# The last two of 231 expert units behind a branch on the routing table

## The chip, the cores and the metric

One core of a Trainium2 chip. The time is the device time of the program in microseconds, the median over several executions; the span is 1.7 to 2.1 us shorter than the time of the same execution. All executions below are on record as fast, none in a slower state. The kernels of this study ran in four jobs, the last three of them on three different chips. One of these is slower than the others by 1.1% (the kernel before takes 1394 us there), so a time is only compared with runs of the kernel before from the same job. A "load" below is the set of runs of one kernel under one label in one job; one execution of each label was traced.

## The reference, cut to what matters

A seven-tap causal convolution along the sequence, with one set of taps for each of 8 groups of channels, makes `attn_out`. A router then picks one expert out of 8 for every token, and the token goes through that expert's two layers.

```python
# batch 8, seq 3584, d_model 192, 8 experts, F = 1024: 28672 tokens, all float32
logits = np.einsum('bsd,de->bse', x, w_gate)
local_gate = 1.0 / (1.0 + np.exp(-np.einsum('bsd,de->bse', x, w_local).squeeze(-1)))
...
        fresh_e = int(np.argmax(logits[b, s]))
        if s == 0 or local_gate[b, s] < 0.5:
            e = fresh_e
        else:
            e = prev_e if prev_e >= 0 else fresh_e
        ...
        h = np.maximum(x[b, s] @ w1[e], 0.0)
        out[b, s] = p[e] * (h @ w2[e])
```

How many tokens an expert gets depends on the data.

## The kernel before

The kernel convolves and routes in 16 groups of 1792 tokens and scatters each routed row into a slot of its expert in a table in memory (`slots`). The slots are worked through in units of 128 rows: 35 single units early, then 87 pairs, then 22 single units at the end (`REST`). The count of 231 covers the worst case, in which each of 8 experts leaves a unit partly filled; a unit that the data does not need gets the entry `DUMMY`, whose rows carry an index out of range.

```python
UT = 128
CAPU = N // UT
NU = (N + E * (UT - 1)) // UT          # 231
DUMMY = E * CAPU
...
    blocks = [(0, 1, i, next(g for g in range(NPART) if i < ONE[g])) for i in range(ONE[-1])]
    blocks += [(1, 2, i, next(g for g in range(NPART) if i < TWO[g])) for i in range(TWO[-1])]
    blocks += [(2, 1, i, NPART - 1) for i in range(REST)]

    def entry(i, col, most):            # SyncE reads the table into a register
        kind, n, at, group = blocks[i]
        return nc.values_load(tabi[kind, group][at:at + 1, col:col + 1], engines=[ET.SP], ...)
    # load_w(i), load_rows(i): DMAs from SyncE, addressed by entry(i, 1, ...) and entry(i, 0, ...)
...
    def hidden(n, wb, xT):              # 48 matmuls for a single unit, then ReLU on ScalarE
    ...
    def output(n, wb, xg, hT):          # 32 matmuls for a single unit
        ...
        for k in range(n):
            nc.scalar.activation(o_sb[:, k, :], y[k][0], Act.Copy, scale=xg[:, k, 0:1])
        step(1.2)
        for k in range(n):
            nc.vector.scalar_tensor_tensor(o_sb[:, k, :], y[k][1], xg[:, k, 0:1], o_sb[:, k, :],
                                           Alu.mult, Alu.add)
            nc.gpsimd.nop()
            sent = nc.gpsimd.indirect_dma_start(out=out, in_=o_sb[:, k, :], ...,
                bounds_check=N - 1, oob_is_err=False)
...
    for i, (_, n, _, _) in enumerate(blocks):
        ensure(i)                       # rows of the next units
        weights(i + AHEAD)              # weights of the next units, 1.5 MB each
        hT = hidden(n, wbs[i], xT)
        if i + 1 < len(blocks):
            xT, copied = turn(blocks[i + 1][1], xgs[i + 1])   # transposes of the next unit
            ...
        output(n, wbs.pop(i), xgs.pop(i), hT)
```

Of the kernel before, what the change touches and what calls it, by code (L numbers as in the profile page):

```python
# [38 lines left out]
NU = (N + E * (UT - 1)) // UT  # L39
DUMMY = E * CAPU  # L40
EARLY = 3


def _sure(tokens, size):

    return max(0, -(-(tokens - E * (size - 1)) // size))



ONE = [_sure(min(g + 1, EARLY) * PT, UT) for g in range(NPART)]  # L50
TWO = [_sure((g + 1) * PT - ONE[-1] * UT, BT) if g >= EARLY else 0 for g in range(NPART)]
REST = NU - ONE[-1] - 2 * TWO[-1]
# [34 lines left out]
def kernel(  # L87
# [8 lines left out]
    nc = tc.nc  # L96
# [173 lines left out]
    tabi = {}  # L270
# [288 lines left out]
    def put(behind=None):  # L559


        if not to_put:
            return
        g, rows, to = to_put.pop(0)
        nc.gpsimd.nop()
        ins = nc.gpsimd.indirect_dma_start(  # L566
            out=slots[:, :], in_=rows, in_offset=None,
            out_offset=bass.IndirectOffsetOnAxis(ap=to, axis=0)).ins
        if behind is not None:
            tc.add_manual_dep(ins, behind.ins.name, SYNC, reason="scatters apart")  # L570
        if puts:
            tc.declare_no_dep(ins, group="puts", reason="slots of their own")
        if g:
            tc.declare_no_dep(ins, group="gets", reason="those slots were full before")
        puts.append((g, ins))
        tc.add_to_no_dep_group("puts", ins)
        tc.add_to_no_dep_group(f"puts{g}", ins)
# [98 lines left out]
    blocks = [(0, 1, i, next(g for g in range(NPART) if i < ONE[g])) for i in range(ONE[-1])]  # L676
# [36 lines left out]
    def turn(n, xg):  # L713


        xps = xps_p.tile([P, 2, 512], F32, name="xps")
        at = xps[:, :, :KD * BT // 2].rearrange("p h (d k s) -> p h d k s", d=KD, k=KT)
        for d in range(KD):
            for k in range(n):
                src = xg[:, k, Y0 + d * DR:Y0 + (d + 2) * DR]  # L720
                for half in range(2):
                    turn_half(at[:, half, d, k, :], src, half)
        xT = tp.tile([P, KD, BT], F32, name="xT")
        to = xT.rearrange("p d (k h s) -> p h d k s", k=KT, h=2)
        if n == KT:
            to, at = [a.rearrange("p h d k s -> p h (d k) s") for a in (to, at)]
        else:
            to, at = [a[:, :, :, 0, :] for a in (to, at)]
        copied = nc.scalar.copy(to, at)  # L729
        return xT, copied  # L730

    def hidden(n, wb, xT):
        hT = hp.tile([P, FK, BT], F32, name="hT")
        w = slice(0, n * P)


        for two in range(2):
            hps = [hps_p.tile([P, 2, BT], F32, name="hps") for half in range(2)]
            for d in range(KD):
                for j in range(2):  # L740
                    f0 = (d * 4 + two * 2 + j) * P
                    for half, rows in halves():
                        nc.tensor.matmul(hps[half][:, j, w], lhsT=wb[rows, f0:f0 + P],  # L743
                                         rhs=xT[rows, d, w], start=(d == 0 and j == 0),
                                         stop=(d == KD - 1), skip_group_check=True)
            for half in range(2):
                m = half * 4 + two * 2
                relu = nc.scalar.activation(hT[:, m:m + 2, w], hps[half][:, :, w], Act.Relu)  # L748
            put(relu)
        return hT  # L750

    def output(n, wb, xg, hT):

        yps = [yps_p.tile([P, 512], F32, name="yps") for half in range(2)]
        for m4 in ([0, 1, 4, 5], [2, 3, 6, 7]):
            for k in range(n):
                for m in m4:
                    for half, rows in halves():
                        nc.tensor.matmul(yps[half][:, k * D:(k + 1) * D],  # L759
                                         lhsT=hT[rows, m, k * P:(k + 1) * P],  # L760
                                         rhs=wb[rows, WA + m * D:WA + (m + 1) * D],
                                         start=(m == 0 and k == 0), stop=(m == FK - 1),
                                         skip_group_check=True)
        o_sb = op.tile([P, KT, D], F32, name="o_sb")
        y = [[yps[half][:, k * D:(k + 1) * D] for half in range(2)] for k in range(n)]
# [9 lines that stand above are left out]
            sent = nc.gpsimd.indirect_dma_start(  # L775
                out=out, in_=o_sb[:, k, :], in_offset=None,
                out_offset=bass.IndirectOffsetOnAxis(ap=xg.bitcast(I32)[:, k, 1:2], axis=0),
                bounds_check=N - 1, oob_is_err=False)
            tc.declare_no_dep(sent.ins, group="sent", reason="each token has one slot")
            tc.add_to_no_dep_group("sent", sent.ins)  # L780
# [5 lines left out]
    def start_conv(on_pe=()):  # L786
        g = st["conv"] + 1

        free = not any(p[0] <= g - 3 for p in to_put)
        if st["cgen"] is None and g < NPART and g <= st["route"] + LEAD and free:  # L790
            st["conv"] = g
            st["cgen"], st["pgen"] = conv(g, x_in.pop(g), on_pe)
            next(st["cgen"])
            if g + 1 < NPART:
                x_in[g + 1] = load_x(g + 1)

    def conv_op():
        c = next(st["cgen"], None) if st["cgen"] else None
        if c is None:
            st["cgen"] = None  # L800
        return c

    def start_route(alone=False):
        done = st["conv"] - (st["cgen"] is not None)
        if st["rgen"] is None and st["route"] < done:
            st["route"] += 1
            st["rgen"] = route(st["route"], alone)

    def route_op():
        c = next(st["rgen"], None)  # L810
        if c is None:
            st["rgen"] = None
            st["routed"] = st["route"]
        return c

    def step(time):

        start_route()
        start_conv()
        go = st["rgen"] is not None  # L820
        while time > 0:
            c = route_op() if go else conv_op()
            if c is None:
                if not go:
                    break
                go = False
            elif c == "hop":
                go = False
            elif c == "placed":
                pass  # L830
            elif c == "pe":
                c = conv_op()
                time -= c or 0
            else:
                time -= c
# [30 lines left out]
    def ensure(i):  # L866

        for j in range(len(xgs) + i, min(i + AHEAD + 1, len(blocks))):
            g = blocks[j][3]
            while st["routed"] < g or any(p[0] <= g for p in to_put):  # L870
                if j > i + 2:
                    return
                step(4.2)
                put()
            xgs[j] = load_rows(j)

    def weights(upto):
        for j in range(loaded[0], min(upto + 1, len(blocks))):
            if (blocks[j][0], blocks[j][3]) not in tabi:
                return  # L880
            wbs[j] = load_w(j)
            loaded[0] += 1

    loaded = [0]
    weights(0)
    for j in range(2):
# [2 lines left out]
    xT, _ = turn(blocks[0][1], xgs[0])  # L889
    for i, (_, n, _, _) in enumerate(blocks):  # L890
        ensure(i)
        weights(i + AHEAD)
        hT = hidden(n, wbs[i], xT)
        if i + 1 < len(blocks):
            xT, copied = turn(blocks[i + 1][1], xgs[i + 1])
            if len(to_put) > NT // 2 and n == KT:
                put(copied)
        step(2.5 if n == 1 else 4.2)
        output(n, wbs.pop(i), xgs.pop(i), hT)
        step(1.3 if n == 1 else 3.0)  # L900


def _w1_layout(np, w1):
# [44 lines left out]
```

## Time and profile before

| | before |
|---|---|
| time | 1378.5 us (three runs, 1378.44 to 1379.59) |
| span of the profiled run | 1377.1 us |
| TensorE busy | 1341.6 us, 97% |
| one single unit of the tail | 5.52 us on TensorE |
| last matmul to the end | 1370.88 to 1377.1 us, so 6.2 us |

The part that matters is the end, and there two intervals: the period of a unit, and the tail between the last matmul and the end. In the tail the last unit is evicted (`o_sb<-yps`, ScalarE and VectorE, 0.42 us each), scattered (GpSimd, 0.97 us), the scatter lands (SyncE's wait for it ends 1.12 us after the scatter's instruction), GpSimd drains (a closing instruction of its sequencer, DRAIN, that in the kernel before begins ahead of the last scatter and ends 3.27 us after it), and a closing barrier joins the engines. The prediction shows the lines.

### The profile page before, as it was taken

The page shows a single profiled execution, that of the slowest core. Times are in us where ns is not written, and L with a number is a line of the kernel's source. Part 1 is how long each engine was busy: PE and PEld are TensorE (multiplying, and loading weights), DVE is VectorE, ACT ScalarE, POOL GpSimd, SP SyncE. Part 2 cuts the span into 40 slices and gives each one's busy share as a digit, 9 for nine tenths or more (in the row PEclk, how much of TensorE's full clock was granted, in tenths as well). Part 3 has the DMA queues.
Part 4 walks back from the last instruction along what each step waited for, and adds up shares of the span by engine and source line. Part 5 has one row for each costly group of instructions (what it writes and reads, how often), then busy time and mean ns, then how long its engine had stood idle before and what let it go on. Part 6 is the DMA issues. An engine that isn't in the chain of part 4 may idle for free.

```text
span 1377.1 us, 42248 instructions
## 1 busy us (share of the span) xinstructions
PE 1341.6 (97%) x17314; PEld 1267.5 (92%) x17314; DVE 794.8 (58%) x2461; ACT 516.0 (37%) x1158; POOL 483.7 (35%) x515
## 2 busy tenths in 40 slices
PE   6789999999999999999999999999999999999998
PEld 4488999999999999999999999999999999999998
DVE  6769999987768686868687778784300000000000
ACT  3234444434333343334333333333333333333333
POOL 1442444434343444444443434343443211112111
PEclk9889999999999999999999999999999999999999
DMA  4299999987676767676767676565665555547993
GB/s 180 100 379 366 379 381 373 365 346 270 207 263 213 263 224 260 229 264 224 263 214 260 213 260 227 204 232 204 225 218 199 195 202 198 180 168 271 320 329 129
DMA packets 66483, 344.16 MB, mean 250 GB/s; under 512 B 12528, under 2 KB 23655, under 8 KB 45810
## 3 DMA queue, kind: packets, MB, share of 16 engines
q1 hardware_dynamic: 44064, 288.76, 58.5%
q0 software_dynamic: 22224, 52.70, 10.1%
q8 instruction: 136, 2.23, 0.6%
q14 instruction: 57, 0.47, 0.1%
q10 hardware_dynamic: 2, 0.00, 0.0%
HBM read 288.61 MB, written 53.49 MB: 248 GB/s over the span
## 4 chain that ended last, share of the span: by engine, by line
PE 62%; issue 22%; DVE 6%; POOL 4%; DMA 4%; ACT 1%; POOLq 0%; SPq 0%; DVEq 0%; ACTq 0%
PE yps L759 28%; PE hps L743 27%; POOL out_dram L775 4%; DVE y_sb L206 3%; DMA xg<-slots 3%; PE xps L278 2%; PE hps L350 2%; PE hps L189 1%; PE yps L189 1%; POOL slots L566 1%; DVE z L340 1%; DVE o_sb L771 1%; DMA x_sb<-in_x_dram 1%; DMA out_dram<-o_sb,xg 0%; ACT z L307 0%
## 5 line engine op out<-in xcount | busy, mean ns | idle before, releaser
L759 PE MATMUL yps<-wb,hT 64*128 64x192 f32 x7392 | 644.0, 326 | 3.2 <-DVE o_sb L771 1.9
L743 PE MATMUL hps<-xT,wb 64*128 64x256 f32 (+1 forms) x6912 | 635.5, 336 | 0.6 <-ACT xT L729 0.6
L759 PEld LDWEIGHTS yps<-wb,hT 64*128 64x128 f32 x7392 | 606.1, 188 | 8.1 <-issue 4.0
L743 PEld LDWEIGHTS hps<-xT,wb 64*128 64x128 f32 x6912 | 573.7, 188 | 39.8 <-ACT xT L729 0.8
L775 POOL DMA_INDIRECT out_dram<-o_sb,xg x231 | 233.5, 1011 | 674.0 <-DVE o_sb L771 601.3
L206 DVE SCALAR_TENSOR_TENSOR y_sb<-x_sb,c,y_sb 128x336 f32<-128x336 f32 x720 | 405.0, 571 | 27.5 <-ACT y_sb L181 8.2
L748 ACT ACTIVATE hT<-hps 128x512 f32<-128x512 f32 (+1 forms) x576 | 263.9, 510 | 364.0 <-PE hps L743 363.8
L771 DVE SCALAR_TENSOR_TENSOR o_sb<-yps,xg,o_sb 128x192 f32<-128x192 f32 x231 | 88.0, 413 | 500.9 <-ACT o_sb L767 495.8
L566 POOL DMA_INDIRECT slots<-y_sb,posi x224 | 223.0, 995 | 185.5 <-ACT hT L748 88.5
L767 ACT ACTIVATE o_sb<-yps,xg 128x192 f32<-128x192 f32 x231 | 87.6, 418 | 425.4 <-PE yps L759 421.8
L729 ACT COPY xT<-xps 128x768 f32<-128x768 f32 (+1 forms) x144 | 97.9, 680 | 10.4 <-PE xps L278 10.4
L278 PEld LDWEIGHTS xps<-ident,xg 64*128 64x128 f32 x1386 | 71.3, 140 | 12.9 <-issue 2.9
L278 PE MATMUL xps<-ident,xg 64*128 64x64 f32 x1386 | 72.8, 222 | 4.9 <-DMA xg<-slots 4.9
L181 ACT ACTIVATE y_sb<-x_sb,c 128x336 f32<-128x336 f32 x116 | 66.7, 586 | 0.0
L340 DVE STREAM_TRANSPOSE z<-y_sb 128x768 f32<-128x768 f32 (+1 forms) x56 | 45.5, 853 | 0.5
L366 DVE COPY lt<-lq 32x36 f32<-32x36 f32 x224 | 41.5, 185 | 3.5
L350 PE MATMUL hps<-z,wg 64*32 64x128 f32 x1344 | 26.9, 274 | 1.9 <-DVE z L340 1.7
L350 PEld LDWEIGHTS hps<-z,wg 64*32 64x32 f32 x1344 | 20.8, 105 | 5.5 <-DVE z L340 3.5
L189 PE MATMUL hps<-x_sb,wb 128*128 128x336 f32 x56 | 18.7, 502 | 3.9 <-DMA x_sb<-in_x_dram 3.9
L189 PEld LDWEIGHTS hps<-x_sb,wb 128*128 128x128 f32 x56 | 12.1, 217 | 10.2 <-issue 5.8
L189 PE MATMUL yps<-x_sb,wb 128*128 128x336 f32 x56 | 19.2, 500 | 0.0
L189 PEld LDWEIGHTS yps<-x_sb,wb 128*128 128x128 f32 x56 | 11.6, 215 | 5.4 <-issue 1.3
(165 smaller groups left out, 336.6 us busy)
## 6 DMA issues: line engine op xcount, KB each, us to landing
wb<-in_w_dram SPq DMA_DIRECT2D x144, 1536.0 KB
x_sb<-in_x_dram SPq DMA_DIRECT2D x16, 1920.0 KB
xg<-slots SPq DMA_DIRECT2D x87, 258.0 KB
xg<-slots SPq DMA_DIRECT2D x57, 129.0 KB
out_dram<-o_sb,xg POOLq DMA_INDIRECT x231
slots<-y_sb,posi POOLq DMA_INDIRECT x224
wg<-in_wgl_dram SPq DMA_DIRECT2D x1, 144.0 KB
slots<-pad SPq DMA_DIRECT2D x1, 129.0 KB
```

The costliest lines, as they stand in the source:

```text
L189: nc.tensor.matmul(acc, lhsT=dg_of(i, k), rhs=chans(h, k), start=(k == 0), stop=(k == KC - 1))
L206: nc.vector.scalar_tensor_tensor(cols(h), chans(h, k), c[:, h, k:k + 1], cols(h), Alu.mult, Alu.add)
L278: nc.tensor.transpose(to, src[rows], identity=ident[rows, rows])
L350: nc.tensor.matmul(lps[half][Q * j:Q * j + Q, :], lhsT=wgq[rows, b, :], rhs=z[rows, begin[j]:begin[j] + TQ, b * Q:(b + 1) * Q], start=(b = ...
L566: ins = nc.gpsimd.indirect_dma_start(out=slots[:, :], in_=rows, in_offset=None, out_offset=bass.IndirectOffsetOnAxis(ap=to, axis=0)).ins
L729: copied = nc.scalar.copy(to, at)
L743: nc.tensor.matmul(hps[half][:, j, w], lhsT=wb[rows, f0:f0 + P], rhs=xT[rows, d, w], start=(d == 0 and j == 0), stop=(d == KD - 1), skip_g ...
L748: relu = nc.scalar.activation(hT[:, m:m + 2, w], hps[half][:, :, w], Act.Relu)
L759: nc.tensor.matmul(yps[half][:, k * D:(k + 1) * D], lhsT=hT[rows, m, k * P:(k + 1) * P], rhs=wb[rows, WA + m * D:WA + (m + 1) * D], start= ...
L767: nc.scalar.activation(o_sb[:, k, :], y[k][0], Act.Copy, scale=xg[:, k, 0:1])
L771: nc.vector.scalar_tensor_tensor(o_sb[:, k, :], y[k][1], xg[:, k, 0:1], o_sb[:, k, :], Alu.mult, Alu.add)
L775: sent = nc.gpsimd.indirect_dma_start(out=out, in_=o_sb[:, k, :], in_offset=None, out_offset=bass.IndirectOffsetOnAxis(ap=xg.bitcast(I32)[ ...
```

## The change

Any routing of 28672 tokens needs 224 to 231 units, so up to seven may be dummies; the last two go behind a branch. All engines read the table entry of the first of them and skip both if it is `DUMMY`.

```diff
--- before.py
+++ after.py
@@ -39,6 +39,7 @@
 NU = (N + E * (UT - 1)) // UT
 DUMMY = E * CAPU
 EARLY = 3
+SPARE = 2
 
 
 def _sure(tokens, size):
@@ -881,6 +882,8 @@
             wbs[j] = load_w(j)
             loaded[0] += 1
 
+    spare = blocks[len(blocks) - SPARE:]
+    del blocks[len(blocks) - SPARE:]
     loaded = [0]
     weights(0)
     for j in range(2):
@@ -898,6 +901,19 @@
         step(2.5 if n == 1 else 4.2)
         output(n, wbs.pop(i), xgs.pop(i), hT)
         step(1.3 if n == 1 else 3.0)
+
+    kind, _, at, group = spare[0]
+    any_left = nc.values_load(tabi[kind, group][at:at + 1, 0:1], min_val=0, max_val=DUMMY,
+                              skip_runtime_bounds_check_because="an entry of the table")
+    with tc.If(any_left < DUMMY):
+        for block in spare:
+            blocks.append(block)
+            i = len(blocks) - 1
+            n = block[1]
+            xg = load_rows(i)
+            wb = load_w(i)
+            xT, _ = turn(n, xg)
+            output(n, wb, xg, hidden(n, wb, xT))
 
 
 def _w1_layout(np, w1):
```

The builder makes two paths of it: the body, and a skip path on which each engine adds to its semaphores what the body would have added, so that later waits can be constants.

## The prediction

> **What bounds the kernel now.** I read the page's first two parts, then the stretches of its last 70 us, then the end in order of time, because the change touches only the end of the program. The busy shares and the slices:
>
> ```profile
> PE 1341.6 (97%) x17314; PEld 1267.5 (92%) x17314; DVE 794.8 (58%) x2461; ACT 516.0 (37%) x1158; POOL 483.7 (35%) x515
> ...
> PE   6789999999999999999999999999999999999998
> ...
> PEclk9889999999999999999999999999999999999999
> ```
>
> TensorE is busy from start to end at almost the full clock, and every other engine has room. So a unit that is not computed gives its whole TensorE time back, if nothing else takes over at the end. What one single unit of the tail costs shows in the last three stretches of 5.52 us (start and end; PE, PEld, DVE, ACT, POOL busy; clock; share of DMA; GB/s):
>
> ```profile
> 1354.24:1359.76 5.52, 5.52 (x91) 5.52 (x88) 0.42 (x1) 2.11 (x6) 0.97 (x1) 1.00 0.27 103
> 1359.76:1365.28 5.52, 5.52 (x90) 5.52 (x89) 0.42 (x1) 2.11 (x6) 0.97 (x1) 1.00 0.06 20
> 1365.28:1370.80 5.52, 5.52 (x85) 5.31 (x82) 0.42 (x1) 1.74 (x5) 0.97 (x1) 1.00 0.01 0
> ```
>
> PE has no gap in them; VectorE works 0.42 us of each, ScalarE 2.11 us. The DMA share falls to nothing because the last weights were asked for at 1349.1 us. The timeline gives the period and the end (start, length, engine):
>
> ```profile
> 1359.76 2.81 PEld L743 LDWEIGHTS hps<-xT,wb 64*128 64x128 f32 x48
> ...
> 1365.28 2.81 PEld L743 LDWEIGHTS hps<-xT,wb 64*128 64x128 f32 x48
> ...
> 1368.11 2.77 PE L759 MATMUL yps<-wb,hT 64*128 64x192 f32 x32
> ...
> 1372.06 0.97 POOL L775 DMA_INDIRECT out_dram<-o_sb,xg  x1 [4.31 <-DVE o_sb L771]
> ```
>
> From one unit's first weight load to the next one's is 5.52 us, and 5.52 again before those shown (1354.24). The last matmul ends at 1370.88, the last scatter's instruction at 1373.03, the program at 1377.1. What lies in those 4.07 us are waits of the closing block, L944 (count; shortest, median, longest in ns; first and last start):
>
> ```profile
> L944 SPq EVENT_SEMAPHORE  x11: 17/28/24651, 1349.5 to 1377.0; - x11
> ...
> L944 POOLq DRAIN  x3: 40/107/4473, 1371.8 to 1376.8; - x3
> ...
> L944 PEldq DRAIN  x2: 13/934/1855, 1369.1 to 1376.6; - x2
> ```
>
> SyncE waits 24.65 us from 1349.5, so until 1374.15, for the last scatter to land. GpSimd's drain is later still: 1371.8 + 4.47 = 1376.3. The barrier behind both takes the rest. GpSimd's drain, not the landing, is what ends the kernel.
>
> **Whether the body will run.** This decides everything. I worked the reference's routing out on the reference's inputs: the experts get 3274, 3841, 3138, 3745, 3518, 3081, 4253 and 3822 tokens, which fill 26 + 31 + 25 + 30 + 28 + 25 + 34 + 30 = 229 units of 128. The program has 231, so exactly the last two are dummies. The trace agrees. The scatters of the last two units moved next to nothing, where the one before moved 0.08 MB (stretches 1359.8 to 1365.3 and 1365.3 to 1371.5; the last one, to 1377.1, has the second line again):
>
> ```profile
> q0 software_dynamic: 48, 0.08, 4.6%
> ```
> ```profile
> q0 software_dynamic: 48, 0.00, 0.5%
> ```
>
> All rows of the last two units carry the row number 28672, which the scatter drops as out of bounds. The branch will skip both.
>
> [...] The page of the kernel before shows the fetches (136 packets of 2.23 MB in all on one queue, so 16 KB each)[...]. [...] 288 such loads from the table on SyncE have a median of 276 ns, and I use that. [...] the last instruction ends at 1373.03, SyncE sees the landing at 1374.15.
>
> **The change part by part.** The instruction order of the changed program is, up to the spare units, the same on each engine as before, waits included, so the first 229 units end exactly two periods earlier than the 231st did.
>
> Removed: two units on TensorE. Each is 48 matmuls of the first product (2.81 us), 32 of the second (2.59 us) and 6 transposes with their share of gaps (0.12 us), 5.52 us; two are 11.04 us. All of it is on the path, as PE has no gap. Also two weight loads of 1.5 MB, two row loads, 10 evictions, 2 VectorE operations and 2 scatters: nothing by themselves, since all lie beside TensorE.
>
> Added on every engine: one register load from the table and one compare-and-branch behind its last real work. [...] VectorE's routing is over by slice 31, about 1070 us, so the table is old and the load waits for nothing. On the skip path each engine then runs a small block that advances the semaphores by what the body would have added. On GpSimd that is a wait for two old scatters and an update of its DMA semaphores (31 ns for the one such instruction in this trace); on SyncE five updates, about 0.06 us apart going by the waits of L944, and long before the end.
>
> Where it lies. Shifted by 11.04, TensorE's last matmul is issued by about 1358 and the barrier is reached at about 1365.3, so TensorE, ScalarE and VectorE have 4 to 5 us of room for load, branch and even a fetch. SyncE has its last weight load behind it by 1338 and waits anyway. Only GpSimd counts: its sequencer reaches the drain 0.24 us before the last scatter begins and 1.2 us before it ends. [...] I expect its end to move little. Booked for this: 0.3 us, an estimate between nothing and a fetch.
>
> Moved: the last scatter is now a real one. The last real one landed about 1.3 us after its instruction (the third last, 1362.24 to 1363.58), the empty ones 1.1 us. If the drain follows the landing, that is 0.2 us.
>
> Sum: 1378.5 - 11.04 + 0.3 + 0.2 = 1368.0 us, 0.76% less.
>
> **The rivals.** (a) A fetch on GpSimd's path. [...] The fetches in this trace are packets of 0.3 to 1 us each, and a first byte as late as the 1.1 us of a landing makes 1.5 to 2.5 us, an estimate. Against it: [...] 1.2 us of it hide behind the scatter. It would make 1369 to 1370. (b) The drain takes its 3.3 us after the scatter's end in full from wherever the sequencer comes to it, or GpSimd's semaphore update queues behind the scatter and SyncE waits for it: 0.5 to 1.5 us more, 1368.5 to 1369.5. (c) The branch costs nothing and the last landing does not matter: 1367.5. (d) The body runs, through a rounding in the routing: then SyncE may ask for its rows and weights only behind the branch, with no prefetch, and TensorE waits for them; some 5 us more than before. Two things speak against it: the empty scatters, and the counts modulo 128, where the total rises above 229 only if, say, expert 7 gained 19 tokens or expert 0 gained 55, and no rounding does that. (e) A different layout of the stream slows the main part. The fetched code up to the branch is the same, so I give it almost nothing.
>
> **Range and chances.** The skip is close to certain and its worth is read off a period that repeats to 0.01 us; what is open is 0 to 2.5 us at the end. Runs of the kernel before spread over 1.2 us. So 1368.0, with 1366.9 to 1369.9 holding it 8 times in 10. Faster by over 2% would need 27.6 us; two units cannot give that. Slower by over 2% needs a fault of the plan. Chances: faster 0.01, within 2% 0.98, slower 0.01.
>
> **What would show it.** PE's busy time falls by about 11 us and its L743 and L759 matmuls by 96 and 64; weight loads from 144 to 142; scatters from 231 to 229; the last matmul ends near 1359.8. The order of time at the end shows GpSimd's load, branch and drain: right if the distance from the last matmul to the end stays near 6.2 us (before: 1377.1 - 1370.88), rival (a) or (b) if it grows to 7.5 or more, with a gap between GpSimd's load and its drain for (a) and none for (b). Wrong altogether if 231 scatters are still there, or if the stretches before 1340 us have another period than 5.52.

## The result, and the profile after

| | runs | median | lowest to highest |
|---|---|---|---|
| before | 6 | 1378.73 us | 1378.44 to 1379.59 |
| changed | 6 | 1366.97 us | 1364.08 to 1368.17 |

The ratio is 0.9912, with a 95% interval of 0.9900 to 0.9925. Here and below a ratio is the mean time of one kernel's fast runs over that of the other's fast runs of the same rounds, so not quite the ratio of the medians quoted. The median lies 0.07 us inside the lower edge of the predicted range, while the means differ by 12.07 us, 1.57 more than the 10.5 that were predicted, and 0.9912 of 1378.5 us is 1366.4, below the range. The gain was larger than predicted.

The page of the changed kernel, first part, shows that the body was skipped: 172 matmuls fewer, which is twice 48 + 32 + 6, two VectorE instructions and two scatters fewer.

```profile
PE 1327.2 (97%) x17142; PEld 1252.3 (92%) x17142; DVE 795.1 (58%) x2459; ACT 512.1 (37%) x1146; POOL 481.2 (35%) x513
```

The last units in order of time (start, length, engine, line, operation) have the same period, 1353.80 - 1348.28 = 5.52 us:

```profile
1348.28 2.81 PEld L744 LDWEIGHTS hps<-xT,wb 64*128 64x128 f32 x48
...
1353.80 2.81 PEld L744 LDWEIGHTS hps<-xT,wb 64*128 64x128 f32 x48
...
1356.63 2.77 PE L760 MATMUL yps<-wb,hT 64*128 64x192 f32 x32
...
1360.58 0.97 POOL L776 DMA_INDIRECT out_dram<-o_sb,xg  x1 [4.31 <-DVE o_sb L772]
```

The last matmul ends at 1359.40 and the program at 1366.07: the tail is 6.67 us, where it was 6.22. What was added stands on the lines of the load, the branch and the closing block (count; shortest, median, longest in ns; first and last start in us):

```profile
L906 POOLq TENSOR_LOAD <-tabi x1: 512/512/512, 1360.3 to 1360.3; - x1
```
```profile
L908 SPq COMPARE_BRANCH  x1: 45/45/45, 1338.4 to 1338.4; - x1
L908 PEldq COMPARE_BRANCH  x1: 477/477/477, 1358.2 to 1358.2; - x1
...
L908 POOLq COMPARE_BRANCH  x1: 53/53/53, 1360.9 to 1360.9; - x1
...
L908 POOLq INC_SWDGE_SEM  x1: 923/923/923, 1361.2 to 1361.2; - x1
```
```profile
L960 POOLq DRAIN  x3: 40/107/3101, 1362.1 to 1365.8; - x3
```

Read GpSimd's part from top to bottom. Its sequencer loads the register and branches around the start of the last scatter (1360.58 to 1361.55), then updates its DMA semaphores for 0.92 us, until 1362.1, and only then does the drain start. That is 0.58 us after the scatter's end, and the drain takes its full 3.10 us from there, until 1365.24. Before, the sequencer stood in the drain from 1371.83, and it ended 3.27 us after the scatter's end. SyncE branched at 1338.4, twenty microseconds ahead of TensorE: each engine takes the branch for itself.

The 11.03 us between the two spans are therefore two periods, 11.04 us, less 0.45 us of longer tail, and 0.45 us that the main part was quicker: the 227th eviction on ScalarE began at 1349.09 before and at 1348.64 after, though up to there the instructions and their waits are the same. So the profiled execution has an excess of 0.45 us over the account. The other five executions were not traced; their mean excess is larger.

### The profile page after: what moved, and what is told of

Its sections match the earlier page's. It is cut to its first block, busy times and chain, and to the rows that moved or that the text cites. A ratio compares the mean times of both kernels' runs of the same rounds, so it can differ in the third digit from the quotient of the medians.

```text
span 1366.1 us, 41871 instructions
## 1 busy us (share of the span) xinstructions
PE 1327.2 (97%) x17142; PEld 1252.3 (92%) x17142; DVE 795.1 (58%) x2459; ACT 512.1 (37%) x1146; POOL 481.2 (35%) x513
## 5 line engine op out<-in xcount | busy, mean ns | idle before, releaser
L760 PE MATMUL yps<-wb,hT 64*128 64x192 f32 x7328 | 636.9, 325 | 3.7 <-DVE o_sb L772 2.0
L760 PEld LDWEIGHTS yps<-wb,hT 64*128 64x128 f32 x7328 | 599.7, 187 | 8.5 <-issue 4.5
L744 PEld LDWEIGHTS hps<-xT,wb 64*128 64x128 f32 x6816 | 567.1, 188 | 41.5 <-issue 1.1
L190 PEld LDWEIGHTS hps<-x_sb,wb 128*128 128x128 f32 x56 | 12.1, 218 | 10.5 <-issue 6.2
```

The source lines that it names most:

```text
L190: nc.tensor.matmul(acc, lhsT=dg_of(i, k), rhs=chans(h, k), start=(k == 0), stop=(k == KC - 1))
L744: nc.tensor.matmul(hps[half][:, j, w], lhsT=wb[rows, f0:f0 + P], rhs=xT[rows, d, w], start=(d == 0 and j == 0), stop=(d == KD - 1), skip_g ...
L760: nc.tensor.matmul(yps[half][:, k * D:(k + 1) * D], lhsT=hT[rows, m, k * P:(k + 1) * P], rhs=wb[rows, WA + m * D:WA + (m + 1) * D], start= ...
```

## The experiments

Two questions were open. What sets the 0.45 us of the tail? And where do the last 1.5 us of the first measurement come from: from scatter between executions (theory A), or from a start that the program with the branch always runs faster (theory B)?

**The changed kernel again, unchanged.**

> The changed kernel once more, unchanged. Both theories name 11.04 us (two unit periods) less 0.4 to 0.5 us of longer tail as what the change itself gives, so 1368.1 to 1368.3 us against 1378.7. Theory A (the 1 to 2 us beyond that in the first measurement are scatter of the first 300 us between executions): the mean of these runs comes closer to 1368.2, within 1366.5 to 1368.7, and the excess over the tail account sits before 300 us in the trace. Theory B (the program with a branch has a start that is faster each time, by its place in memory or its fetches): again 1366.0 to 1367.0, the spread again 2 us or more.

Measured: 1384.76 us median (1381.40 to 1385.93, 6 runs) against 1394.4 us (1390.87 to 1398.48, 11 runs), ratio 0.9927, interval 0.9911 to 0.9943. This was the slower chip, so the expected absolute times do not apply, the differences do: the means differ by 9.9 us, not 12. The tail is 6.67 us. The kernel before is anything but steady on this chip; its runs span 7.6 us. This speaks for A, though the interval is too wide to rule B out. Where A expected the difference from the account, in the first 300 us, it is only in part (see "Where the scatter sits").

**Two units dropped, no branch.** On these inputs the result stays right, on others it would not.

```diff
-    spare = blocks[len(blocks) - SPARE:]
     del blocks[len(blocks) - SPARE:]
...
-    any_left = nc.values_load(...)
-    with tc.If(any_left < DUMMY):
-        ...
```

> 229 units and no branch at all (right on these inputs alone). Account of the tail: two periods less and no tail cost, 1378.7 - 11.04 = 1367.7, that is 0.4 to 0.5 us less than the changed kernel, with the distance from the last matmul to the end at 6.2 to 6.4 us. Theory A: its main part scatters like that of the others, mean within 1366 to 1368. Theory B: 1367.5 to 1368 with a narrow spread like the kernel before, because it has no branch.

Measured: 1382.47 us median (5 runs) against the same 1394.4, ratio 0.9910, interval 0.9894 to 0.9926. The tail is 6.07 us, 0.60 less than with the branch, as the account of the tail has it (GpSimd's drain there, in ns and us as above):

```profile
L946 POOLq DRAIN  x3: 40/107/4310, 1375.7 to 1380.5; - x3
```

The drain starts at 1375.67, before the last scatter (1375.91 to 1376.88), and ends at 1379.98, 3.10 us after it. In the kernel before this was 3.27 us behind an empty scatter. So the real scatter at the end makes the tail 0.15 us shorter, where the prediction made it 0.2 us longer, and the branch costs 0.60 us of tail. In the time, this kernel came out 2.6 us below the changed one by the means, more than the tails explain. It has no branch and yet gained as much as the changed kernel did the first time, where B expected the account's value and a narrow spread.

**The branch alone.** All 231 units stay in the loop; the same branch and body stand behind them and the body never runs.

```diff
     spare = blocks[len(blocks) - SPARE:]
-    del blocks[len(blocks) - SPARE:]
```

> All 231 units in the loop and behind them the same branch with the same body, which never runs: the cost of the branch alone. Account of the tail: 0.4 to 0.5 us above the kernel before, 1379.1 to 1379.3, with GpSimd's semaphore update of 0.9 us in front of its drain. Theory A: main part scatters, 1377.5 to 1379.5. Theory B: 1.5 us faster than that, 1377 to 1378, with a spread of 2 us or more.

Measured: 1394.22 us median (5 runs), ratio 1.0000, interval 0.9984 to 1.0016. The interval reaches 2.2 us to either side, so a cost below a microsecond cannot be seen in the time of this chip. In the trace the tail is 7.20 us, 0.98 more than before, where 0.4 to 0.5 were expected: 0.6 by the later drain, and the rest mostly a gap of 0.3 us between GpSimd's last drain and its last barrier step, which the changed kernel's trace does not have (0.04 to 0.13 us there) and which I did not pursue. Theory B expected a kernel about 1 us faster than the one before, with a spread of 2 us or more: the means are 0.2 us apart the other way and the spread is 2.05 us, which decides nothing within that interval. TensorE brought a surprise:

```profile
L907 PEldq COMPARE_BRANCH  x1: 3575/3575/3575, 1385.2 to 1385.2; - x1
...
L907 POOLq INC_SWDGE_SEM  x1: 977/977/977, 1388.2 to 1388.2; - x1
```

The same branch over the same body took TensorE 0.48 us in the changed kernel and 3.58 here. Within it lies a fetch of instructions, in the window from 1385 to 1389 us:

```profile
q8 instruction: 1, 0.02, 1.9%
```

One packet of 16 KB, at 1386.28, 1.03 us after the branch began. In the changed kernel none lies within TensorE's branch (1358.23 to 1358.71); its next one starts at 1359.56. The packets do not say for which engine they are, so that TensorE waited for this one is inferred. Why one falls within the branch here and none there was not shown. TensorE had time for it: it reached the barrier at 1389.0 and GpSimd's drain ended at 1392.5.

**The kernel before under a label of its own.**

> The kernel before, once more, under its own label: the noise floor between two loads of one program. Theory A: ratio to the kernel before within 0.1 per cent but single runs 1 to 4 us apart if enough of them are taken; Theory B: within 0.05 per cent and a spread near 1 us, as in its first six runs.

Measured: 1393.64 us median, 1390.56 to 1397.30 over 6 runs, ratio 0.9997. One load of one program scatters by 6.7 us, so theory B's narrow kernel before does not hold on this chip. The time is within what both theories expected of it.

**The branch without scatters in its body.** The body never runs, so the result is right here; it would be wrong where the body is needed.

```diff
+            if not send:
+                continue
             nc.gpsimd.nop()
             sent = nc.gpsimd.indirect_dma_start(
...
-            output(n, wb, xg, hidden(n, wb, xT))
+            output(n, wb, xg, hidden(n, wb, xT), send=False)
```

> As the changed kernel, but the body behind the branch leaves out its two scatters (it never runs, so the result stays right). The skip path on GpSimd then has load and branch but no DMA semaphore update. Theory of the update (the 0.9 us update in front of GpSimd's drain is all of the branch's cost): from the last matmul to the end 6.07 us as without a branch, 0.6 us less than the changed kernel's 6.67, and the drain begins before the last scatter ends. Rival (the register load and the branch themselves hold the end up): 6.5 us or more even so. In the time 0.6 us less than the changed kernel, which the scatter between runs may hide.

Measured: 1365.91 us median (4 runs) against 1378.54 (9 runs, 1376.07 to 1379.48), ratio 0.9912. The tail is 6.11 us. GpSimd still loads and branches, but has no update, and the drain starts at 1359.3, before the scatter ends at 1359.80:

```profile
L961 POOLq DRAIN  x3: 40/113/3571, 1359.3 to 1363.5; - x3
```

So the update costs 0.56 us of tail, and all the rest of the branch 0.04, which lies behind the drain and not in the load or the branch (the drain ends 3.11 us after the scatter, as without a branch). This is rival (b) of the prediction: in the changed kernel the drain took its 3.10 us in full from where the sequencer came to it, 1362.14. Whether the update queues behind the scatter, the second form of (b), stays open: in the changed kernel's trace it begins at 1361.18, during the scatter, and ends 0.55 us after it. In the time this version came out 2.3 us below the changed kernel of the same job, by the means; that is more than the 0.56 us of the tail, and in its trace the start of the program was the quickest of the nine compared below.

**The branch in front of the last real unit**, with buffers of its own for the body.

```diff
         weights(i + AHEAD)
+        if i + 1 == len(blocks):
+            behind_branch()             # load, tc.If, body with pools tp2 and hp2
         hT = hidden(n, wbs[i], xT)
```

> The same branch and body, but in front of the last real unit instead of behind it (with its own buffers for the transposed rows and the hidden layer). Theory of the update: the tail falls back to 6.07 us, because the update is long done. In its place TensorE must stand still in mid-stream: its register load and branch took 0.5 and 0.4 to 0.5 us, and its semaphore update waits until the last matmul is through, so a gap of 0.3 to 1.5 us in front of the last unit. Net 0.3 us less to 0.9 us more than the changed kernel. Rival: branches are hidden by the queues here too, no gap, and the kernel is 0.6 us faster than the changed one.

Measured: 1370.19 us median (5 runs), ratio 0.9949, so 2.1 us over the changed kernel of the same job (below) by the medians and 2.8 by the means. The tail fell to 5.98 us (6.07 expected), but TensorE lost more in mid-stream than I had allowed for:

```profile
1349.72 2.59 PEld L762 LDWEIGHTS yps<-wb,hT 64*128 64x128 f32 x32
1355.09 4.39 PEld L746 LDWEIGHTS hps<-xT,wb 64*128 64x128 f32 x47 [2.77 <-issue]
```
```profile
L894 PEldq COMPARE_BRANCH  x1: 3361/3361/3361, 1351.4 to 1351.4; - x1
```
```profile
1355.10:1360.60 5.50, 5.48 (x62) 5.50 (x63) 0.00 (x0) 1.32 (x4) 0.00 (x0) 0.69 0.07 21
```

Again one 16 KB packet of instructions lies within the branch, 1.00 us after its start, and the gap is 2.77 us. In the traces of the changed kernel (the first and the third), of the version without scatters and of the one with the branch before the eviction TensorE's branch took 0.48 to 0.49 us; in the first of these no such packet lies within it. Behind the gap the granted clock is 0.69 on average (the third figure from the end of the last line), which is 3.4 of the 5.50 us at half clock, the only lower value in the clock records of the kernels before and after; 47 weight loads took 4.39 us, where 48 took 2.81 in the changed kernel.

**Three units behind the branch.** The third last is real here, so the body runs.

```diff
-SPARE = 2
+SPARE = 3
```

> Three units behind the branch instead of two: the third last is a real one on these inputs, so the body runs, all three units. What a wrong guess costs. One theory: SyncE branches for itself as soon as its queue is through, so rows and weights come early all the same, and what is lost is the overlap inside each unit (transpose, copy and hidden layer one after the other): 1 to 2 us a unit, 3 to 6 us over the kernel before. Rival (d) of the prediction: no prefetch, TensorE waits for rows and weights, 5 us or more for the first unit and 8 to 15 in all. The first 228 units take what they took.

Measured: 1380.94 us median (4 runs) against 1378.54, ratio 1.0019, interval 1.0003 to 1.0034 (against all nine runs of the kernel before the means are 3.15 us apart). That is the lower edge of the 3 to 6 us of the first theory, and the trace has its mechanism. TensorE's weight loads in the body:

```profile
1355.01 0.37 PEld L279 LDWEIGHTS xps<-ident,xg 64*128 64x128 f32 x6
1356.58 2.76 PEld L744 LDWEIGHTS hps<-xT,wb 64*128 64x128 f32 x48 [1.20 <-ACT xT L730]
...
1361.81 0.37 PEld L279 LDWEIGHTS xps<-ident,xg 64*128 64x128 f32 x6
1363.22 2.76 PEld L744 LDWEIGHTS hps<-xT,wb 64*128 64x128 f32 x48 [1.04 <-ACT xT L730]
```

A unit takes 1361.81 - 1355.01 = 6.80 us in place of 5.52, and what TensorE waits for is ScalarE's copy of the transposed rows, not a DMA. SyncE had passed the branch at 1334.3 and had asked for all rows and weights of the body by 1350.5. Rival (d), no prefetch, is wrong. Between the three units of the body a wrong guess costs 1.1 to 1.3 us a unit.

**The changed kernel a third time**, in the job of the last three.

> The changed kernel a third time. Theory A (scatter): the ratio lies anywhere within 0.9905 to 0.994 with a mean over the three loads near 0.9923 (10.6 us less), the tail is 6.67 us again, and all that differs from that account sits in the first part of the trace. Theory B (a faster start each time): 0.991 or less.

Measured: 1368.11 us median (1367.71 to 1369.17, 5 runs), ratio 0.9927, tail 6.68 us. The interval, 0.9914 to 0.9941, excludes the 0.991 or less of theory B: theory A holds.

**A version meant to beat both.** The branch stands between the matmuls of the last real unit and its eviction, and the body takes other buffers in PSUM for what the matmuls write (`hps` in place of `yps`).

```diff
+        if between is not None:
+            between()                   # load, tc.If, body with PSUM from hps_p
         o_sb = op.tile([P, KT, D], F32, name="o_sb")
```

> A version meant to beat both: the branch stands between the last real unit's matmuls and its eviction and scatter, with other PSUM buffers for the body. Every engine then loads, branches and updates its semaphores while it has to wait anyway; GpSimd is idle over 4 us before the last scatter. Theory of the update: the tail is 6.07 us as without a branch, the distance to the changed kernel 0.6 us, the ratio to the kernel before near 0.9919. Rival (a branch costs on TensorE or through a fetch wherever it stands): tail 6.5 us or more; should TensorE's branch take 3.4 us for a fetch here, it still ends before the barrier.

Measured: 1367.40 us median (1364.67 to 1371.02, 6 runs) against 1377.65 (11 runs, 1376.42 to 1379.04), ratio 0.9924, interval 0.9911 to 0.9937. The tail is 6.11 us as expected. The update has moved behind the scatter of the unit before and ends 3.5 us ahead of the drain:

```profile
L895 POOLq INC_SWDGE_SEM  x1: 909/909/909, 1357.6 to 1357.6; - x1
```
```profile
L967 POOLq DRAIN  x3: 40/113/4317, 1362.0 to 1366.9; - x3
```

So the branch is all but free in the tail (6.07 us without one). It is meant to be correct for any routing, but no run here entered this version's body. The time does not show the gain: 0.56 us is lost in this kernel's scatter of 6.4 us, and its mean is 0.1 us above that of the changed kernel beside it.

**The changed kernel a fourth time, beside it.**

> The changed kernel beside it on the same chip, for the comparison: tail 6.67 us, ratio 0.9923 by the account of two periods less 0.45 us, scatter between 0.991 and 0.994.

Measured: 1367.63 us median (5 runs), ratio 0.9924, tail 6.66 us.

**Two units dropped, again beside it.**

> 229 units without a branch once more: tail 6.07 us, ratio 0.9919 by the account. Its first load came out at 0.991, 2.5 us below the changed kernel of the same chip where the traces' tails differ by 0.6; scatter says the gap to the changed kernel is back near 0.6 us, within 2 us of it to either side.

Measured: 1366.30 us median (5 runs), ratio 0.9919, tail 6.07 us. The means are 1.2 us below the changed kernel's, within 2 us as expected; the 2.6 us of the first time were scatter for the most part.

**Where the scatter sits.** All these programs run the same instructions up to the branch or the missing units. The 37th copy of transposed rows on ScalarE is a mark in the middle of the program; its start in the traces of the three faster jobs, first the kernel before, then the changed kernel (the job of the first measurement), then the version without scatters in the body and the one with the branch before the eviction:

```profile
296.94 0.81 ACT L729 COPY xT<-xps 128x768 f32<-128x768 f32 x1
```
```profile
296.35 0.81 ACT L730 COPY xT<-xps 128x768 f32<-128x768 f32 x1
```
```profile
294.16 0.81 ACT L730 COPY xT<-xps 128x768 f32<-128x768 f32 x1
```
```profile
298.08 0.81 ACT L730 COPY xT<-xps 128x768 f32<-128x768 f32 x1
```

Nine such traces lie between 294.16 and 298.08 us. From that mark to the 227th eviction they need 1051.4 to 1052.7 us. So most of the spread of 3.8 us between them (at the 227th eviction) is made in the first 297 us, where convolution, routing, scatters and units share the engines, and TensorE runs at half clock for 14 to 24 us; and programs with a branch are found at both ends. What in the first 297 us makes it stays open: the time at half clock does not order the traces (20.5 us of it went with 296.94, with 298.08 and with 294.16 alike). On the slower chip it is otherwise: its four traces reach the mark within 309.0 to 310.0 us and then need 1054.1 to 1056.6 us, so more of the spread lies behind the mark. The changed kernel's trace there is 3.5 us longer than the account gives from the trace of the kernel before under its own label; 1.0 us of that lies before the mark and 2.5 behind it.

## Why the prediction was right or wrong

That the body is skipped, and what the skip is worth, held. The step that failed is "the first 229 units end exactly two periods earlier than the 231st did", and the width of the range that was built on it.

- *The body is skipped.* Right: 229 scatters, 142 weight loads, 172 matmuls fewer.
- *Two periods of 5.52 us.* Right: the period is the same after, and the same in the traces without the two units.
- *TensorE's busy time falls by about 11 us.* It fell by 14.4. Of the 3.4 us beyond the units, 2.9 lie before 297 us (76.38 + 191.30 us busy there before, 74.32 + 190.49 after), where the clock was at half for 20.5 us before and for 13.7 after.
- *Other engines and SyncE have room.* Right: even the branch of 3.58 us on TensorE had ended 3.65 us before the drain did that ends the kernel.
- *0.3 us for load, branch and update on GpSimd.* The mechanism was taken wrong. The register load took 0.51 us there, not the 0.28 that SyncE's loads had suggested, which did no harm. The branch's share was my estimate, as the trace before holds no branch; GpSimd's took 53 ns. I booked the update at 31 ns, from the one at the start of the program, and let the drain begin before the scatter ends. Behind a scatter the update takes 0.92 us, the drain began 0.58 us after the scatter and took its full 3.10 us: 0.60 us, of which 0.56 are the update's. Rival (b) had it, but the prediction's sign for it, a tail of 7.5 us or more, did not show: the tail of 6.67 us lies between that and the 6.2 that meant right.
- *0.2 us for a real last scatter.* Wrong sign: 0.15 us less, from 3.27 to 3.10 us of drain.
- Together the last two were 0.5 us predicted and 0.45 measured; two errors that cancelled.
- *The main part, "exactly two periods earlier".* This is the step that failed. In the traced pair the last matmul ended 1370.89 - 1359.40 = 11.49 us earlier, not 11.04, and over the six runs the means leave 1.5 us beyond the account. The prediction booked nothing for this: what was open it put at the end of the program, it gave rival (e), a slower main part, almost nothing and a quicker one no place at all, and for scatter it took "Runs of the kernel before spread over 1.2 us. So 1368.0, with 1366.9 to 1369.9 holding it 8 times in 10." Three runs of one load had happened to agree. Loads of the same kernel before later spread over 3.4 us (9 runs), 2.6 (11), 7.6 (11) and 6.7 (6), the changed one over 4.1, 4.5, 1.5 and 2.3. The account, 11.04 - 0.45 = 10.6 us or a ratio of 0.9923, lies within the interval of each of its four loads: 0.9912, 0.9927, 0.9927, 0.9924, mean 0.9922. The excess of the first load, 1.5 us, is of the size of that scatter, and no other load of the changed kernel repeated it, so I put it down to scatter of the main part between executions; as only one of its six executions was traced, this is argued from the later loads rather than seen in the first, and what makes the main part scatter stays open.
- *Rival (a), a fetch on GpSimd's path*, did not occur: its branch took 53 ns and the next step followed 0.14 us later. On TensorE two programs show a fetch within a long branch (3.36 and 3.58 us). The prediction's "packets of 0.3 to 1 us" was a misreading: the 136 packets of that queue take 0.88 to 1.61 us, median 0.97.

## What to carry to other kernels

Skipping work that the data does not need gave back its time on the bounding engine here, 11.04 us; the branch itself was cheap where each engine met it while it would wait anyway (0.04 us of tail without the update), and dear on the bounding engine in mid-stream (a gap of 2.77 us). Look at what the skip path has to do for the semaphores, not only at the branch: here the one GpSimd update was 0.56 of the 0.60 us that the branch cost in the tail, and moving the branch in front of the last eviction hid it (a tail of 6.11 us against 6.07 without a branch). And take the width of a range from several loads of a kernel, not from three runs of one.

## What the runs show of branches, loads and drains

- A compare-and-branch took 45 to 50 ns on SyncE, 45 on ScalarE, 53 on GpSimd and 72 on VectorE where the body is skipped; on TensorE 477 to 490 in four traces there, and 3361 and 3575 in the two programs with a fetch during the branch. In the run whose body ran TensorE's two took 87 and 180 ns.
- These two long branches are about 3 us more on TensorE, with one 16 KB packet of instructions during the branch, and none during that of the changed kernel. That TensorE waited for the packet is inferred.
- Loading a register from the table took a median of 276 ns on SyncE in the kernel before (265 to 660), and 476 to 552 ns on the other engines in the changed kernel.
- The run with the branch before the last unit shows a granted clock of 0.69 over the 5.50 us behind a gap of 2.77 us between two weight loads (2.51 between matmuls, whose ends are modelled).
- Updating GpSimd's DMA semaphores took 0.91 to 0.98 us in five traces, and 31 ns at the start of the kernel before. GpSimd's drain took 3.10 us behind that update in the changed kernel, ended 3.10 us after the real last scatter where two units were dropped, and 3.27 us after the scatter that drops all its rows in the kernel before.
